# First batch's plain value rows loaded as float32 by SyncE and cast by VectorE, with the plain heads' products and the first FFN tiles reordered

## The chip, the cores and the metric

The kernel runs on one core of a Trainium2 chip. The time is the device time in microseconds of that core. A profile of one execution stands beside it; its span, 311.4 us, runs from the first to the last instruction and is a little shorter than the time. The granted TensorE clock was 1.000 throughout.

## The reference

Eight batches of windowed attention over 576 tokens, eight heads of 64; the first four heads ("plain") see the last 32 tokens, the other four ("dilated") every fourth of the last 128. The result, laid out as tokens by 512, goes through a two-layer network with a squared ReLU.

```python
B, H, S, D = q.shape                      # 8, 8, 576, 64
scores = scale * np.matmul(q, k.transpose(0, 1, 3, 2))
rel = pos[:, None] - pos[None, :]
mask_plain = (rel >= 0) & (rel < 32)
mask_dil = (rel >= 0) & (rel < 32 * 4) & (rel % 4 == 0)
masks = np.stack([mask_plain if h < H // 2 else mask_dil for h in range(H)], axis=0)
attn = softmax(np.where(masks, scores, -1e9))
x = np.matmul(attn, v).transpose(0, 2, 1, 3).reshape(B * S, H * D)   # 4608 x 512
h = np.maximum(x @ w_in, 0.0)             # 512 x 2048
out = (h * h) @ w_out                     # 2048 x 512
```

All inputs and outputs are float32. The kernel computes in bf16 with float32 sums.

## The kernel before

All of the order is fixed by hand. A string, PROGRAM, lists small steps; a "|" stands for the next FFN group. Heads are taken in pairs e: pairs 0 and 1 are plain, 2 and 3 dilated. The first batch is cut into part 0 (tokens 0 to 255) and part 1 (256 to 575). For pair e and part p the steps are: T transposes q and k on TensorE, C copies them out of PSUM, B starts an accumulator with the mask's bias, S adds the scores, E takes the exponential on ScalarE, P multiplies with the values, D sums the denominators, L and X take their logarithm and the exponential of its negative on ScalarE, M multiplies into xT on VectorE. "w9" and "W2" are matmuls on idle operands that keep TensorE occupied. "L0:" codes are loads of the first batch by GpSimd: q (with k), v in parts, i0 to i3 the four pieces of w_in, o0 to o3 those of w_out.

```python
PROGRAM = (
    "L0:q001 L0:q023 L0:q101 L0:q123 L0:v0d L0:v0p L0:i0 L0:v1dr L0:i1 L0:v1p L0:i2 L0:i3 L0:o0 L0:o1 L0:o2 "
    "L0:o3 L1:q00123 z y L1:v0dp L1:q10123 L1:v1dpr w9 T00 C00a T10 C10a B00 B10 S00 E00 B20 S10 E10 B30 T20q "
    "B01 W2 T20k C20v T30 C30v B11 W1 S20 E20 W1 S30 E30 T01 C01v T11 C11v W1 S01 E01 T21 C21v B21 S11 E11 T31 "
    "C31v P20 P30 D20 D30 L20 X20 M20 P00 P10 D00 D10 L00 X00 M00 B31 S21 E21 S31 E31 W2 | | P21 P31 D21 D31 "
    "L21 X21 M21 L31 X31 M31 | | P01 P11 D01 D11 L01 X01 M01 L11 X11 M11 | | | | | | | | | | | | | m n | | | | "
    # ... later batches
)
```

The values of the first batch. "p" are those of the plain heads, cast by the DMA into their places in `vbd`; "d" those of the dilated heads; "r" the last 64 tokens of the dilated heads.

```python
def load_v(b: int, parts, which="pdr"):
    dst = vbd[b % 2]
    # ...
    for what in which:
        if what == "p":
            for e in range(NE // 2):
                for hl, rows in sides:
                    nc.gpsimd.dma_start(                                   # L178
                        dst[rows, e, i0:i1, rows],
                        v[b, 2 * e + hl, 64 * i0 : 64 * i1, :].rearrange("(i p) d -> p i d", p=64),
                    )
        # ... "d" into vds (L184)
        elif p1 == 2:
            for hl, rows in sides:
                nc.gpsimd.dma_start(                                       # L197
                    dst[rows, NE // 2 : NE, 8, rows],
                    v[b, H // 2 + hl : H : 2, 512:S, :].rearrange("h p d -> p h d"),
                )
```

The first layer of the FFN. A tile of 256 tokens has eight accumulators u, each of eight matmuls (two column blocks, four rows kt of x; row kt is pair kt). Accumulators 0 and 1 need piece 0 of w_in, 2 and 3 piece 1, and so on. Accumulators, score banks and some products share the four PSUM buffers of `ps_f`. The h2T step takes ReLU on ScalarE and squares on VectorE.

```python
def ffn_groups(tk0: int, nt: int):
    early = 0 < tk0 <= 2 * NT
    # ...
    kts = (0, 2, 1, 3) if tk0 >= NT else (2, 3, 0, 1)
    cut = 3 if tk0 >= NT else 2

    def mm1(u, ks):
        if u not in acc:
            acc[u] = ps_f.tile([P, NT], f32, name="pf")
        # ... matmuls of the rows ks                                         L668
        hv = h2[:, per * u : per * u + per, 0:nt]
        nc.scalar.activation(hv, acc[u][:, :].rearrange("p (x n) -> p x n", x=per), ACT.Relu)   # L679
        nc.vector.tensor_tensor(out=hv, in0=hv, in1=hv, op=ALU.mult)                             # L680

    def g1(i):
        if i < 2 and early:
            for u in (2 * i, 2 * i + 1):
                mm1(u, kts[:cut])
        elif i < 4 and early:
            for u in (2 * i - 4, 2 * i - 3):
                mm1(u, kts[cut:])
        else:
            mm1(i, kts)
    # ... g2: the second layer (L700), copy to osb (L706), store by SyncE (L642)

head = groups[:G]        # 0..15: tile 0 (tokens 0-255), 16..31: tile 1 (tokens 256-511)
groups[:NF] = [head[y] for y in (0, 1, 2, 3, 16, 17, 18, 19, 4, 5, 20, 21, 6, 7, 22, 23)]
```

Of the kernel before, what the change touches and what calls it, by code (L numbers as in the profile page):

```python
# [21 lines left out]
    "L0:q001 L0:q023 L0:q101 L0:q123 L0:v0d L0:v0p L0:i0 L0:v1dr L0:i1 L0:v1p L0:i2 L0:i3 L0:o0 L0:o1 L0:o2 "  # L22
    "L0:o3 L1:q00123 z y L1:v0dp L1:q10123 L1:v1dpr w9 T00 C00a T10 C10a B00 B10 S00 E00 B20 S10 E10 B30 T20q "
    "B01 W2 T20k C20v T30 C30v B11 W1 S20 E20 W1 S30 E30 T01 C01v T11 C11v W1 S01 E01 T21 C21v B21 S11 E11 T31 "
    "C31v P20 P30 D20 D30 L20 X20 M20 P00 P10 D00 D10 L00 X00 M00 B31 S21 E21 S31 E31 W2 | | P21 P31 D21 D31 "
    "L21 X21 M21 L31 X31 M31 | | P01 P11 D01 D11 L01 X01 M01 L11 X11 M11 | | | | | | | | | | | | | m n | | | | "
    "| L2:q00123 L2:q10123 | 1q1 1q3 | 1q2 1k2 | 1k1 1v3 | 1a2 | 1v2 1k0 1q0 | 1o2 | 1a0 1a1 | 1k3 1o0 1o1 | "
    "1a3 1Q0 | 1K0 1o3 | 1Q1 1K1 | 1Q2 | 1b0 | | 1Q3 1K2 L2:vwpdr L3:q00123 L3:q10123 | L2:x | | 2q0 | | 2k0 "
    "1V2 | 1b2 1p0 | 1b1 1V3 1K3 | | 1p2 1p1 | 2a0 1b3 | 2k1 2o0 2b0 1p3 | 2q1 2k2 L3:x | | 2q2 2p0 L3:vwpdr "
    "2a1 | | | 2b1 | 2o1 2q3 2a2 | | 2p1 2v2 | 2k3 | 2b2 2o2 | 2v3 | 2a3 2p2 L4:q10123 | 2b3 3k1 | 2o3 3q1 | | "  # L30
    "3a1 L4:q00123 2p3 | 3k0 3k2 | | 3o1 | | | 3q0 3v2 | | | | 3a0 | 3b1 3k3 | | | 3p1 L4:x 3q2 L4:vwpdr | | "  # L31
    "3b0 | 3a2 3q3 3o0 4k0 | | | 3o2 3b2 | | 3p0 3v3 | 4q1 3a3 | 3p2 4q2 4q0 | L5:q10123 3b3 | 3o3 | 4k1 | | "
# [31 lines left out]
def kernel(  # L64
# [9 lines left out]
    nc = tc.nc  # L74
    P = nc.NUM_PARTITIONS
    B, H, S, D = q.shape
# [378 lines left out]
    first = {}  # L455
    sides = [slice(64 * hl, 64 * hl + 64) for hl in range(2)]

    def turn(n: int, cols: int):


        if "W" not in first:
            pool, nm = (ps_f, "pf") if ("P", 2, 0) in first else (ps_o, "po")
            first["W"] = pool.tile([P, 512], f32, name=nm)
        for _ in range(n):
            nc.tensor.matmul(
                first["W"][:, 0:cols], idle[:, 0:P],
                idle[:, 0:256].unsqueeze(1).broadcast_to([P, cols // 256, 256]), start=True, stop=True, skip_group_check=True
            )

    def first_step(code: str):  # L470
# [91 lines left out]
        elif what == "P":  # L562
            if ("P", *pair) not in first:
                if pair in ((2, 0), (2, 1), (0, 1)):
                    od = ps_o.tile([P, 512], f32, name="po"), ps_d.tile([P, 512], f32, name="pd")
                else:
                    od = [ps_a.tile([P, 512], f32, name="pa") for _ in range(2)]
                first.pop("W", None)
                first["P", *pair] = od
# [75 lines left out]
    def ffn_groups(tk0: int, nt: int):  # L645
# [3 lines left out]
        early = 0 < tk0 <= 2 * NT  # L649
        h2 = h2_pool.tile([P, NF, NT], bf16, name="h2T")  # L650
        per = NT // nt
        kts = (0, 2, 1, 3) if tk0 >= NT else (2, 3, 0, 1)
# [29 lines left out]
        def g1(i):  # L682
            if i < 2 and early:
                for u in (2 * i, 2 * i + 1):
                    mm1(u, kts[:cut])
            elif i < 4 and early:
# [4 lines that stand above are left out]
# [76 lines left out]
    def run(code):  # L767
# [7 lines left out]
        elif code == "m":  # L775
            masks()
        elif code == "n":
            zero_halves(kbd)
            zero_halves(vbd[0][:, NE // 2 :, 0:8, :])
        elif code[0] in "wW":  # L780
            turn(int(code[1:]), 512 if code[0] == "w" else 256)
# [26 lines left out]
    groups[:NF] = [head[y] for y in (0, 1, 2, 3, 16, 17, 18, 19, 4, 5, 20, 21, 6, 7, 22, 23)]  # L808
# [54 lines left out]
```

## Time and profile before

| | |
|---|---|
| time, median of 3 | 313.79 us (313.38 to 313.93) |
| span in the profile | 311.4 us |
| TensorE busy | 300.0 us, 96% |
| ScalarE, VectorE busy | 196.9 us, 193.7 us |
| GpSimd busy | 96.3 us, nearly all of it issuing loads |
| second layer's first matmul (L700) starts | 35.07 us |

A timeline line gives the start, the time from the start to the end of a run of like instructions, the engine, the source line, the operation with its operands and shape, the count, and in brackets how long the engine had been idle just before and what ended that idleness. A matmul's end is modelled, so starts are the thing to compare. GpSimd's load lines are the issues alone. The landings of the first loads, from the trace's DMA answer (issue plus time to landing):

| load | KB written | issued, us | landed after, us |
|---|---|---|---|
| q, first | 128 | 1.25 | 3.3 |
| q, third load (pairs 2, 3) | 128 | 2.60 | 5.1 |
| k of pairs 2, 3, part 1 (eighth) | 160 | 5.70 | 6.1 |
| plain values, part 0, first of four | 32 | 7.99 | 4.8 |
| w_in piece 0 (fifteenth) | 512 | 11.41 | 5.7 |
| w_in piece 1 | 512 | 14.48 | 6.9 |
| w_in piece 2 | 512 | 18.68 | 7.4 |
| w_in piece 3 | 512 | 19.71 | 9.0 |

### The profile page before, as it was taken

The page shows a single profiled execution, that of the slowest core. Times are in us where ns is not written, and L with a number is a line of the kernel's source. Part 1 is how long each engine was busy: PE and PEld are TensorE (multiplying, and loading weights), DVE is VectorE, ACT ScalarE, POOL GpSimd, SP SyncE. Part 2 cuts the span into 40 slices and gives each one's busy share as a digit, 9 for nine tenths or more (in the row PEclk, how much of TensorE's full clock was granted, in tenths as well). Part 3 has the DMA queues.
Part 4 walks back from the last instruction along what each step waited for, and adds up shares of the span by engine and source line. Part 5 has one row for each costly group of instructions (what it writes and reads, how often), then busy time and mean ns, then how long its engine had stood idle before and what let it go on. Part 6 is the DMA issues. An engine that isn't in the chain of part 4 may idle for free.

```text
span 311.4 us, 6742 instructions
## 1 busy us (share of the span) xinstructions
PE 300.0 (96%) x2532; PEld 186.1 (60%) x2564; DVE 193.7 (62%) x631; ACT 196.9 (63%) x420; POOL 96.3 (31%) x142
## 2 busy tenths in 40 slices
PE   7989999999999999999999999999999999999994
PEld 3769746968755555565599555555555555445443
DVE  1445567998978879974898469946994334104400
ACT  7377738859878865785388547854786456226511
POOL 8879785664236254501451041000000000000000
PEclk9999999999999999999999999999999999999999
DMA  8999999999999969999699976502200210121022
GB/s 108 153 182 211 206 148 180 174 127 221 153 101 194 175 107 204 155 101 199 98 132 115 173 126 90 101 10 61 67 2 1 69 68 0 36 67 34 2 67 67
DMA packets 79808, 34.91 MB, mean 112 GB/s; under 512 B 49824, under 2 KB 74784, under 8 KB 79776
## 3 DMA queue, kind: packets, MB, share of 16 engines
q0 software_dynamic: 47680, 18.36, 53.4%
q1 hardware_dynamic: 31952, 15.93, 28.8%
q8 instruction: 20, 0.33, 0.5%
q10 hardware_dynamic: 144, 0.20, 0.2%
q14 instruction: 12, 0.10, 0.2%
HBM read 36.90 MB, written 9.44 MB: 149 GB/s over the span
## 4 chain that ended last, share of the span: by engine, by line
PE 81%; ACT 5%; DMA 5%; DVE 2%; POOL 2%; issue 2%; SPq 0%; ACTq 0%; POOLq 0%
PE pf L668 36%; PE pf L700 36%; PE po L413 3%; PE pd L415 2%; DMA w_in<-in_moe_w_in_dram 2%; DMA qb<-in_q_dram 2%; PE pa L304 2%; ACT h2T L679 1%; PE pa L310 1%; ACT qT L248 1%; DMA out_dram<-osb 1%; PE pa L235 1%; ACT osb L706 1%; DVE xT L428 1%; DVE kbd L252 1%
## 5 line engine op out<-in xcount | busy, mean ns | idle before, releaser
L668 PE MATMUL pf<-xT,w_in 128*128 128x256 bf16 (+1 forms) x758 | 132.7, 325 | 2.9 <-DMA w_in<-in_moe_w_in_dram 1.4
L700 PE MATMUL pf<-w_out_sb,h2T 128*128 128x512 bf16 (+1 forms) x570 | 130.9, 373 | 1.7 <-ACT osb L706 0.5
L668 PEld LDWEIGHTS <-w_in 128*128 128x128 bf16 x768 | 82.3, 114 | 38.3 <-issue 1.9
L679 ACT ACTIVATE h2T<-pf 128x512 bf16<-128x512 f32 x144 | 83.8, 598 | 25.1 <-PE pf L668 24.2
L700 PEld LDWEIGHTS <-h2T 128*128 128x128 bf16 x592 | 54.3, 98 | 53.9 <-issue 0.7
L680 DVE TENSOR_TENSOR h2T<-h2T 128x512 bf16<-128x512 bf16 x144 | 58.1, 423 | 41.5 <-ACT h2T L679 39.9
L706 ACT COPY osb<-pf 128x512 f32<-128x512 f32 (+1 forms) x37 | 21.2, 572 | 42.2 <-PE pf L700 42.1
L428 DVE TENSOR_TENSOR xT<-po,rec 128x288 bf16<-128x288 f32 (+2 forms) x52 | 23.7, 456 | 30.5 <-ACT rec L418 30.0
L178 POOL DMA_DIRECT2D vbd<-in_v_dram x40 | 28.2, 725 | 43.0 <-PE pd L415 39.6
L417 ACT ACTIVATE rec<-pd 128x288 f32<-128x288 f32 (+2 forms) x52 | 21.5, 413 | 24.0 <-PE pd L415 21.5
L314 ACT ACTIVATE pt<-pa 128x352 bf16<-128x352 f32 (+6 forms) x56 | 27.6, 499 | 8.4 <-PE pa L310 4.7
L418 ACT ACTIVATE rec<-rec 128x288 f32<-128x288 f32 (+2 forms) x56 | 24.9, 444 | 1.8
L413 PEld LDWEIGHTS <-vbd 128*128 128x128 bf16 x286 | 16.8, 97 | 9.9 <-issue 0.7
L248 DVE COPY qT<-xx 64x288 bf16<-64x288 bf16 x80 | 19.4, 243 | 1.8 <-DMA xx<-qb 0.7
L191 POOL DMA_DIRECT2D vd<-in_v_dram x24 | 14.6, 624 | 15.1 <-DMA kb<-in_k_dram 8.1
L252 DVE COPY kbd<-xx 64x288 bf16<-64x288 bf16 x40 | 18.8, 470 | 0.6
L161 POOL DMA_DIRECT2D qb<-in_q_dram x18 | 13.0, 720 | 18.8 <-DMA xx<-qb 17.1
L413 PE MATMUL po<-pt,vbd 128*128 128x96 bf16 (+3 forms) x263 | 18.0, 199 | 0.3 <-DVE vbd L207 0.2
L415 PE MATMUL pd<-pt,mk 128*128 128x96 bf16 (+5 forms) x158 | 16.3, 203 | 0.0
L197 POOL DMA_DIRECT2D vbd<-in_v_dram x16 | 9.6, 608 | 12.3 <-PE pd L415 5.1
L161 POOL DMA_DIRECT2D kb<-in_k_dram x18 | 12.8, 709 | 2.0 <-PE pf L415 1.1
L304 PE MATMUL pa<-qT,kbd 128*128 128x96 bf16 (+2 forms) x146 | 12.2, 201 | 0.5 <-ACT qT L248 0.5
(82 smaller groups left out, 230.4 us busy)
## 6 DMA issues: line engine op xcount, KB each, us to landing
out_dram<-osb SPq DMA_DIRECT2D x18, 128.0 KB, 3.4
qb<-in_q_dram POOLq DMA_DIRECT2D x7, 320.0 KB, 7.3
kb<-in_k_dram POOLq DMA_DIRECT2D x7, 320.0 KB, 8.0
vd<-in_v_dram POOLq DMA_DIRECT2D x32, 64.0 KB, 6.2
w_in<-in_moe_w_in_dram POOLq DMA_DIRECT2D x4, 512.0 KB, 7.2
w_out_sb<-in_moe_w_out_dram POOLq DMA_DIRECT2D x4, 512.0 KB, 12.9
qb<-in_q_dram POOLq DMA_DIRECT2D x7, 256.0 KB, 7.0
kb<-in_k_dram POOLq DMA_DIRECT2D x7, 256.0 KB, 8.7
```

The source lines that it names most:

```text
L161: nc.gpsimd.dma_start(t[0:n, part, hs, :], src[b, hs, t0 : t0 + RES * n, :].rearrange("h (p r) d -> p h (r d)", r=RES))
L178: nc.gpsimd.dma_start(dst[rows, e, i0:i1, rows], v[b, 2 * e + hl, 64 * i0 : 64 * i1, :].rearrange("(i p) d -> p i d", p=64),)
L314: nc.scalar.activation(pt[:, off : off + n], ps[:, 0:n], ACT.Exp, scale=SCALE)
L413: nc.tensor.matmul(oo, vb[:, e, i, :], rh, start=(x == 0), stop=(x == len(mms) - 1), skip_group_check=True)
L415: nc.tensor.matmul(dd, ones[:, :], rh, start=(x == 0), stop=(x == len(dms) - 1), skip_group_check=True)
L418: nc.scalar.activation(rec[:, 0:n], rec[:, 0:n], ACT.Exp, scale=-1.0)
L428: nc.vector.tensor_tensor(out=tok, in0=o if o is o3 else o[:, 0:n], in1=rec if o is o3 else rec[:, 0:n], op=ALU.mult)
L668: nc.tensor.matmul(acc[u][:, nt * x + y0 : nt * x + y1], w_in_sb[piece][:, kt, c0 : c0 + 509 : 4], xT[:, kt, t0 : t0 + y1 - y0], start=(kt ...
L679: nc.scalar.activation(hv, acc[u][:, :].rearrange("p (x n) -> p x n", x=per), ACT.Relu)
L680: nc.vector.tensor_tensor(out=hv, in0=hv, in1=hv, op=ALU.mult)
L700: nc.tensor.matmul(cur[m][:, c0:c1], h2[:, f, P * m : P * m + P], w_out_sb[:, f, c0:c1], start=(f == 0), stop=(f == NF - 1),)
L706: nc.scalar.copy(osb[:, c0:c1], cur[m][:, c0:c1])
```

## The change

The plain heads' values of the first batch, and the last 64 tokens of the dilated heads, no longer come through GpSimd's queue with a cast. SyncE, which has nothing to do until the first stores at 41 us, loads them as float32 into the three `osb` buffers that later hold output rows, and VectorE casts them into `vbd`. A tiny memset on VectorE ahead of each set fixes when the loads may start. With the ten issues out of GpSimd's queue, w_in moves ahead in it. Since the plain values are meant to be there early, the plain heads' products of part 0 (P00 ... M00) are taken before those of the dilated ones. The first two FFN tiles follow suit: each one's first two accumulators are filled with two rows of x first and the other two in the next group, tile 0 in the order plain, dilated, tile 1 in the order dilated, plain.

```diff
-    "L0:q001 L0:q023 L0:q101 L0:q123 L0:v0d L0:v0p L0:i0 L0:v1dr L0:i1 L0:v1p L0:i2 L0:i3 L0:o0 L0:o1 L0:o2 "
-    "L0:o3 L1:q00123 z y L1:v0dp L1:q10123 L1:v1dpr w9 T00 C00a T10 C10a B00 B10 S00 E00 B20 S10 E10 B30 T20q "
-    "B01 W2 T20k C20v T30 C30v B11 W1 S20 E20 W1 S30 E30 T01 C01v T11 C11v W1 S01 E01 T21 C21v B21 S11 E11 T31 "
-    "C31v P20 P30 D20 D30 L20 X20 M20 P00 P10 D00 D10 L00 X00 M00 B31 S21 E21 S31 E31 W2 | | P21 P31 D21 D31 "
-    "L21 X21 M21 L31 X31 M31 | | P01 P11 D01 D11 L01 X01 M01 L11 X11 M11 | | | | | | | | | | | | | m n | | | | "
+    "L0:q001 L0:q023 L0:v0d L0:q101 L0:q123 L0:i0 L0:v1d L0:i1 L0:i2 L0:i3 L0:o0 L0:o1 L0:o2 L0:o3 L1:q00123 z "
+    "y L1:v0dp L1:q10123 L1:v1dpr w9 T00 C00a g0 T10 C10a B00 B10 S00 E00 B20 S10 E10 B30 W2 T20q T20k C20v "
+    "T30 C30v h0 W3 S20 E20 W1 S30 E30 P00 P10 D00 D10 L00 X00 T01 C01v g1 M00 T11 C11v B01 B11 P20 P30 D20 "
+    "D30 L20 X20 M20 S01 T21 C21a T31 C31v E01 S11 E11 | B21 S21 E21 h1 | B31 S31 E31 P21 P31 D21 D31 L21 X21 "
+    "M21 L31 X31 M31 P01 P11 D01 D11 L01 X01 M01 L11 X11 M11 | | | | | | | | | | | | | | | m n | | | | | "
 # ... later batches: the same steps, wrapped elsewhere
+    plain = {}
+    def load_plain(part: int):                       # codes g0, g1
+        if part == 0:
+            plain[0] = t = osb_pool.tile([P, DM], f32, name="osb")
+            nc.vector.memset(t[:, 0:512:256], 0.0)
+            to = [t[:, 256 * e : 256 * e + 256] for e in range(2)]
+        else:
+            plain[1] = ts = [osb_pool.tile([P, DM], f32, name="osb") for _ in range(2)]
+            for t in ts:
+                nc.vector.memset(t[:, 0:448:64], 0.0)
+            to = [t[:, 0:320] for t in ts]
+            for hl, rows in enumerate(sides):
+                nc.sync.dma_start(
+                    ts[0][rows, 320:448].rearrange("p (h d) -> p h d", d=D),
+                    v[0, H // 2 + hl : H : 2, 512:S, :].rearrange("h p d -> p h d"),
+                )
+        for e in range(2):
+            for hl, rows in enumerate(sides):
+                nc.sync.dma_start(
+                    to[e][rows, :].rearrange("p (i d) -> p i d", d=D),
+                    v[0, 2 * e + hl, 256 * part : 256 + 320 * part, :].rearrange("(i p) d -> p i d", p=64),
+                )
+    def cast_plain(part: int):                       # codes h0, h1
+        for rows in sides:
+            if part == 0:
+                x = plain[0][rows, :].rearrange("p (e i d) -> p e i d", e=2, d=D)
+                nc.vector.tensor_copy(vbd[0][rows, 0:2, 0:4, rows], x)
+            else:
+                x = plain[1][0][rows, 320:448].rearrange("p (e d) -> p e d", d=D)
+                nc.vector.tensor_copy(vbd[0][rows, 2:4, 8, rows], x)
+                for e in range(2):
+                    x = plain[1][e][rows, 0:320].rearrange("p (i d) -> p i d", d=D)
+                    nc.vector.tensor_copy(vbd[0][rows, e, 4:NB, rows], x)
 # ... the idle matmuls (W) always in ps_o
-                    od = [ps_a.tile([P, 512], f32, name="pa") for _ in range(2)]
+                    pool, nm = (ps_a, "pa") if part else (ps_f, "pf")
+                    od = [pool.tile([P, 512], f32, name=nm) for _ in range(2)]
-        early = 0 < tk0 <= 2 * NT
+        early = NT <= tk0 <= 2 * NT
-        kts = (0, 2, 1, 3) if tk0 >= NT else (2, 3, 0, 1)
+        kts = (0, 2, 1, 3) if tk0 >= NT else (0, 1, 2, 3) if tk0 == 0 else (2, 3, 0, 1)
         def g1(i):
-            if i < 2 and early:
+            if i < 2 and tk0 < NT:
+                for u in range(2):
+                    mm1(u, kts[2 * i : 2 * i + 2])
+            elif i < 2 and early:
-    groups[:NF] = [head[y] for y in (0, 1, 2, 3, 16, 17, 18, 19, 4, 5, 20, 21, 6, 7, 22, 23)]
+    groups[:NF] = [head[y] for y in (0, 1, 16, 2, 3, 17, 18, 19, 4, 5, 20, 21, 6, 7, 22, 23)]
```

In the built programs nothing else moves: after the head each engine has the same instructions in the same order, GpSimd has ten issues fewer, SyncE ten more, VectorE three memsets and eight casts more, and the copy C21 goes from VectorE to ScalarE.

## The prediction

> **What bounds the kernel now.** I read the page first, then stretches of five microseconds, then TensorE's timeline and the chain of waits of the first 45 us. The page's engine table and its row of slices show where there is anything to win.
>
> ```profile
> PE 300.0 (96%) x2532; PEld 186.1 (60%) x2564; DVE 193.7 (62%) x631; ACT 196.9 (63%) x420; POOL 96.3 (31%) x142
> ...
> PE   7989999999999999999999999999999999999994
> ```
>
> TensorE is busy 96% of 311.4 us at full clock, and from 100 to 300 us, which the change leaves alone, the stretches give it 99.31 and 99.40 of each 100 us. The first 35 us are what can change; they end where the first second-layer matmul (L700) starts, at 35.07 us. TensorE's timeline from 15 us (start, duration, then in brackets the idle time before and who ended it):
>
> ```profile
> 15.89 0.39 PE L465 MATMUL pf<-idle 128*128 128x256 bf16 x2
> 17.14 2.16 PE L668 MATMUL pf<-xT,w_in 128*128 128x256 bf16 x16 [0.85 <-DMA w_in<-in_moe_w_in_dram]
> 19.23 0.46 PE L587 MATMUL po<-pt,vd 64*64 64x32 bf16 x16
> ...
> 21.45 1.94 PE L668 MATMUL pf<-xT,w_in 128*128 128x256 bf16 x16 [0.53 <-DMA w_in<-in_moe_w_in_dram]
> ...
> 26.45 8.79 PE L668 MATMUL pf<-xT,w_in 128*128 128x256 bf16 x79 [0.30 <-DVE xT L620]
> 35.07 6.21 PE L700 MATMUL pf<-w_out_sb,h2T 128*128 128x512 bf16 x27
> ```
>
> Two waits are for pieces of the first weight (0.85 and 0.53 us), one for x (0.30). Before 15 us there are gaps of 0.26, 0.20, 0.30 and 0.18 us and seven idle-operand fillers worth about 0.2 us each. Together some 4 us, 1.3% of the run, is the most that any reordering here can give. From 26.45 to 41 us TensorE does not wait: 79 matmuls in 8.62 us, 0.109 us each.
>
> GpSimd's timeline says why the weights are late:
>
> ```profile
> 9.14 1.83 POOL L178 DMA_DIRECT2D vbd<-in_v_dram  x3 [0.52 <-DMA kb<-in_k_dram]
> 11.41 0.76 POOL L752 DMA_DIRECT2D w_in<-in_moe_w_in_dram  x1 [0.44 <-DMA qb<-in_q_dram]
> ```
>
> Its queue reuses eight semaphores, so each load waits for the landing of the one eight places earlier (the program's waits show it). Piece 0 of w_in is the fifteenth load, is issued at 11.41 us and lands 5.7 us later, at 17.1. The DMA answer for 2 to 22 us, in half-microsecond slices, shows the queues starving ahead of it:
>
> ```profile
> GB/s 264 59 83 187 188 120 84 77 114 152 171 168 174 185 180 186 193 190 198 136 92 40 35 53 205 209 205 209 190 180 203 199 198 209 207 172 151 154 143 167
> ```
>
> From 12 to 14 us the rate is 92, 40, 35 and 53 GB/s, against 205 next to it. Part of that is the plain values' 128-byte packets; I put the rest, a true hole, at 1.3 us. Otherwise the queues are full from 2.5 us to the end of the weights, so order in the stream decides landings.
>
> **What the Trainium skill says.** "DMA: Bandwidth & Descriptors", section "SWDGE vs HWDGE vs iDMA": a cast in a DMA is to be had on GpSimd only; hence float32 staging and a VectorE cast. Its section "Issuing engines are not separate DMA queues" says that all issuers share the same 16 engines and interleave, so a second queue saves issue time only. The profile before has no SyncE load beside GpSimd's to test it, but it fits the full stream. "VectorE: DVE Perf Modes", "The perf-mode tier table": a float32 SBUF copy of 2048 elements takes 1227 ns, twice the plain rate; my estimate for 512 is 0.43 us (0.27 of streaming and 0.16 fixed). No such copy is in the trace. "SBUF — State Buffer", "SBUF: two separate sides", warns that such a copy locks GpSimd out of writing descriptors; here it could delay only issues that are already ahead of the stream.
>
> **Part by part.** *Loads.* Ten GpSimd issues go (8 of 725 ns, 2 of 608 ns in the page's means: 7.0 us). w_in piece 0 becomes the eleventh load and waits for the third, which lands 5.1 us after 2.60: issue at about 7.7 us instead of 11.41, and the hole closes. In exchange SyncE brings the same values as float32: 256 KB in four loads and 384 KB in six, twice the written bytes, in 256-byte packets. The first four start after a VectorE memset behind the first k copy (6.4 us). Before, only the first set stood ahead of piece 0; the second set came after piece 1. Now the second set is issued at about 13 us by my chain below and shares the engines with piece 0's last part. Landing of piece 0: 17.1 - 1.3 (hole) + 0.3 (wider writes) = 16.1 us, up to 0.6 more if the second set gets in.
>
> *Attention's first part.* To the last plain exponentials nothing moves; scores of pairs 2 and 3 end at about 10.5 us. P00 then needs both casts. The fourth SyncE load is issued near 8 us; with the 2.3 us that the mask load on ScalarE's queue takes alone, and some sharing, it lands near 10.6, and two casts of 0.43 us end at 11.3: a new wait of 0.8 us. P00 to D10 take 0.62 (as at 14.23 before), L00 and X00 1.2 on ScalarE, M00 0.7: x of the plain heads is there at 13.9 us instead of 17.55. T01, T11, B01, B11, pairs 2 and 3's products, S01, T21, T31 and S11 follow, 3.4 us of TensorE work with small waits: the first FFN group is ready at about 15.3 us. So it waits for the weight, and t = 16.1.
>
> *From t on.* The first two groups now hold 16 matmuls (rows 0,1 then 2,3 of two accumulators): 1.75 us. Between and after stand B21, S21, B31, S31 (1.3), the products and sums of pairs 2 and 3 (19.23 to 20.73: 1.5) and of 0 and 1 (23.22 to 24.12: 0.9). Then comes tile 1's first group, which needs rows 2,3 of x: M21 and M31. Two waits arise. ScalarE takes E31 after two squaring inputs h2T, so P31 waits 0.3 us. And L21, X21, L31, X31, M31 take 2.3 us from D21's end (20.73 to 23.02 before), while TensorE has only D31 and the 0.9 us of P01 to D11: it waits about 1.4 us. Before, two FFN groups (1.94 us) stood in that place. So t + 1.75 + 1.3 + 1.5 + 0.9 + 0.3 + 1.4 = t + 7.15 to tile 1's first group, then 112 matmuls at 0.109 = 12.2, and 0.2 for an accumulator bank: t + 19.5. Break-even with 35.07 is t = 15.6; with t = 16.1 the mark is reached at 35.6, 0.5 us later. After that the order is unchanged and TensorE full, so the shift is kept: 313.79 + 0.5 = 314.3 us.
>
> **Rivals.** (1) Piece 0 lands as early as TensorE is ready, 15.3 us or before, because the queues' packets overlap better than in one queue; then the mark is 34.8 or less. If the 1.4 us behind M31 is also smaller, 1 to 1.5 us are won: 312.4. For it speaks the hole and the fact that x of plain heads comes 3.6 us earlier; against it, 640 KB of float32 ahead of or beside piece 0, where before 128 KB of bf16 stood ahead of it. (2) The SyncE loads are slow among the full queues: the fourth lands at 12, P00 starts at 12.8, q and k of part 1 land a microsecond later too, and t becomes 17: 315.2. For it: out stores of 128 KB took 5.9 us to land in this stretch. (3) The head is only exchanged, TensorE being short of w_in piece 1 either way (0.53 us before): then nothing, 313.8. Against it: piece 1's first use moves behind tile 1's group, to about t + 8, after 24 us, and its landing (21.4 before) leaves slack.
>
> **Range and chances.** t may lie between 15.1 and 17.1 and the waits behind it may be off by 0.6, which gives about 34.0 to 36.7 for the mark; the run-to-run spread (313.38 to 313.93) adds little. I lean a little to the early side, since I may have put the loads too strictly in line: 312.8 to 315.5. Two per cent is 6.3 us; only 4 us can be won, and losing 6 would need TensorE to stand still for all that the loads can be late. So within 2%: 0.98, 0.01 on each side.
>
> **What would show it.** First L668 between 15.3 and 17 us, its idle time ended by w_in; P00 waiting for VectorE's cast; no slice under 100 GB/s between 12 and 14 us; tile 1's first group waiting for the multiply of M31 (an idle of over 1 us ended by VectorE); the first L700 at 35.6. Wrong if the first L668 starts before 15, if P00 follows S30 at once, or if a stretch after 40 us differs by more than 0.3 us.

## The result and the profile after

| | before | after |
|---|---|---|
| time, median of 4 | 313.86 us (313.38 to 314.21) | 336.90 us (335.85 to 337.27) |
| span in the profile | 311.4 us | 335.0 us |
| mean granted TensorE clock | 1.000 | 0.979 |
| second layer's first matmul starts | 35.07 us | 58.42 us |

The change makes the kernel slower: the ratio is 1.073, with a 95% interval of 1.0702 to 1.0758. The prediction was 314.3 us (312.8 to 315.5) and was wrong by 22.6 us. The span grew by 23.6 us, and the mark at which the second layer starts moved by 23.35 us. So nearly all of the loss is made ahead of that mark, where the prediction had placed what can change.

The page of the changed kernel: the engine table, and the rows of 40 slices (one is 8.4 us) for TensorE and for its granted clock.

```profile
PE 310.5 (93%) x2563; PEld 191.7 (57%) x2563; DVE 197.6 (59%) x641; ACT 198.0 (59%) x421; POOL 90.1 (27%) x132
...
PE   8375289999999999999999999999999999999995
PEclk9999569999999999999999999999999999999999
```

TensorE's busy share falls to 3, 7, 5 and 2 tenths in slices 2 to 5 (8.4 to 42 us), where it had been 8 or 9. In the fifth and sixth slice the clock is at five and six tenths.

TensorE's timeline of the changed kernel, 18 to 59 us (start, time to the end of the run, engine, line, operation, count; in brackets the idle time before and who ended it):

```profile
18.53 0.77 PE L627 MATMUL pf<-pt,vbd 128*128 128x96 bf16 x8 [6.87 <-DVE vbd L486]
...
25.38 1.89 PE L708 MATMUL pf<-xT,w_in 128*128 128x256 bf16 x8
...
29.58 0.44 PE L627 MATMUL po<-pt,vd 64*64 64x32 bf16 x16
39.84 0.23 PE L627 MATMUL po<-pt,vbd 128*128 128x64 bf16 x1 [9.82 <-DVE vbd L489]
...
42.84 0.56 PE L627 MATMUL po<-pt,vbd 128*128 128x32 bf16 x6 [1.13 <-DVE xT L660]
...
44.41 14.17 PE L708 MATMUL pf<-xT,w_in 128*128 128x256 bf16 x112
58.42 1.89 PE L743 MATMUL pf<-w_out_sb,h2T 128*128 128x512 bf16 x8
```

Two waits stand out. P00 waits 6.87 us and P21 waits 9.82 us, each for a cast of values that SyncE loads (L486 is the cast of the first set, L489 that of the dilated rows in the second, L492 that of its plain rows). Before, neither waited at all:

```profile
14.23 0.48 PE L587 MATMUL pa<-pt,vbd 128*128 128x96 bf16 x8
...
19.76 0.19 PE L587 MATMUL po<-pt,vbd 128*128 128x64 bf16 x1
```

The first FFN group (25.38) waits for nothing: w_in is there by then. From the start of the 112 matmuls at 44.41 to the mark it is 14.01 us, where the prediction had 12.2: they begin at half speed.

A cast is short. VectorE's timeline shows that it is itself kept waiting, by the load:

```profile
16.89 0.42 DVE L486 CAST vbd<-osb 64x512 bf16<-64x512 f32 x1 [6.55 <-DMA osb<-in_v_dram]
18.05 0.42 DVE L486 CAST vbd<-osb 64x512 bf16<-64x512 f32 x1 [0.73 <-DMA osb<-in_v_dram]
21.28 0.08 DVE L467 MEMSET osb<- 128x7 f32 x2
29.55 0.22 DVE L489 CAST vbd<-osb 64x128 bf16<-64x128 f32 x1 [3.68 <-DMA osb<-in_v_dram]
36.34 0.48 DVE L492 CAST vbd<-osb 64x320 bf16<-64x320 f32 x1 [6.57 <-DMA osb<-in_v_dram]
39.05 0.48 DVE L492 CAST vbd<-osb 64x320 bf16<-64x320 f32 x1 [2.23 <-DMA osb<-in_v_dram]
39.56 0.22 DVE L489 CAST vbd<-osb 64x128 bf16<-64x128 f32 x1
```

P21 itself needs only the dilated rows, the two casts of L489. Their loads had landed by 31.8 us, but the second of these casts stands behind two of L492 in VectorE's order, and those wait for the plain rows, which landed between 36.3 and 40.4 us. That order is not what costs the time: P01, two products later, needs the plain rows anyway. e1 below shows it: there P21 goes 2.76 us earlier, P01 waits longer, and the mark does not move.

The chain of work that ended last, in order of time (start, duration, what), says the same from the other side:

```profile
8.95 9.00 DMA osb<-in_v_dram
...
21.38 0.59 SPq L470
...
24.05 14.91 DMA osb<-in_v_dram
```

One load of the first set takes 9.00 us and one of the second 14.91 us. These two stretches are 23.9 us of the first 40. They also stand in line: the memsets that start the second set (L467, at 21.28 in the timeline above) lie behind x copies that need TensorE, and TensorE had stood until 18.53. So the second set is issued at 21.38 us; the prediction had it at about 13.

Are the DMA engines idle meanwhile? The DMA answer of the changed kernel for 0 to 45 us (40 slices of 1.125 us, then the median time from issue to landing):

```profile
GB/s 0 57 148 173 125 117 174 164 148 154 192 206 190 189 196 204 207 206 207 206 209 230 199 223 209 211 217 203 219 202 190 182 183 184 184 160 152 173 135 171
...
osb<-in_v_dram SPq DMA_DIRECT2D x4, 80.0 KB, 14.6
...
osb<-in_v_dram SPq DMA_DIRECT2D x4, 64.0 KB, 8.2
```

They are not: from 11 to 34 us they move 189 to 230 GB/s. The hole that the prediction wanted closed is closed. What they move, though, is mostly something else than the 640 KB that everyone waits for.

### The profile page after: what moved, and what is told of

Same layout as the page of the kernel before. It is cut to its first block, busy times and chain, and to the rows that moved or that the text cites. A ratio compares the mean times of both kernels' runs of the same rounds, so it can differ in the third digit from the quotient of the medians.

```text
span 335.0 us, 6792 instructions
## 1 busy us (share of the span) xinstructions
PE 310.5 (93%) x2563; PEld 191.7 (57%) x2563; DVE 197.6 (59%) x641; ACT 198.0 (59%) x421; POOL 90.1 (27%) x132
## 4 chain that ended last, share of the span: by engine, by line
PE 80%; DMA 7%; ACT 5%; DVE 4%; issue 2%; SPq 1%; ACTq 0%; DVEq 0%
PE pf L708 35%; PE pf L743 34%; DMA osb<-in_v_dram 7%; PE po L413 3%; PE pd L415 2%; PE pa L304 2%; PE po L505 1%; PE pa L310 1%; ACT h2T L719 1%; ACT qT L248 1%; PE pa L235 1%; SPq L476 1%; DVE kbd L252 1%; DVE xT L428 1%; ACT rec L417 1%
## 5 line engine op out<-in xcount | busy, mean ns | idle before, releaser
L708 PE MATMUL pf<-xT,w_in 128*128 128x256 bf16 (+1 forms) x768 | 136.2, 331 | 0.6 <-DVE xT L428 0.3
L743 PE MATMUL pf<-w_out_sb,h2T 128*128 128x512 bf16 (+1 forms) x592 | 134.5, 373 | 0.5 <-ACT osb L749 0.5
L708 PEld LDWEIGHTS <-w_in 128*128 128x128 bf16 x768 | 83.3, 115 | 37.4 <-issue 1.2
L749 ACT COPY osb<-pf 128x512 f32<-128x512 f32 (+1 forms) x37 | 21.2, 573 | 42.2 <-PE pf L743 40.0
L178 POOL DMA_DIRECT2D vbd<-in_v_dram x32 | 23.1, 742 | 77.8 <-PE pd L415 57.3
L413 PEld LDWEIGHTS <-vbd 128*128 128x128 bf16 x286 | 16.9, 97 | 10.2 <-issue 1.0
L248 DVE COPY qT<-xx 64x288 bf16<-64x288 bf16 x80 | 20.1, 251 | 1.1
L304 PE MATMUL pa<-qT,kbd 128*128 128x96 bf16 (+2 forms) x146 | 12.2, 201 | 0.5 <-ACT qT L248 0.5
L627 PEld LDWEIGHTS <-vbd 128*128 128x128 bf16 x22 | 1.7, 131 | 18.3 <-DVE vbd L489 9.9
## 6 DMA issues: line engine op xcount, KB each, us to landing
w_in<-in_moe_w_in_dram POOLq DMA_DIRECT2D x4, 512.0 KB, 11.7
```

Of the source, the lines that this page charges most:

```text
L178: nc.gpsimd.dma_start(dst[rows, e, i0:i1, rows], v[b, 2 * e + hl, 64 * i0 : 64 * i1, :].rearrange("(i p) d -> p i d", p=64),)
L248: copy(qT[rows, e, :, m0 : m0 + n].rearrange("p (c j) m -> p j c m", j=2)[:, jj, :, :], src)
L413: nc.tensor.matmul(oo, vb[:, e, i, :], rh, start=(x == 0), stop=(x == len(mms) - 1), skip_group_check=True)
L708: nc.tensor.matmul(acc[u][:, nt * x + y0 : nt * x + y1], w_in_sb[piece][:, kt, c0 : c0 + 509 : 4], xT[:, kt, t0 : t0 + y1 - y0], start=(kt ...
L743: nc.tensor.matmul(cur[m][:, c0:c1], h2[:, f, P * m : P * m + P], w_out_sb[:, f, c0:c1], start=(f == 0), stop=(f == NF - 1),)
```

## The theories

**Theory of turns.** The DMA engines serve SyncE's queue and GpSimd's in turn, one packet each. SyncE's packets are of 256 bytes. GpSimd's are of 512 bytes for q and k (59 ns each in the trace), 1024 for w_in (96 ns) and 4096 for w_out (322 ns). While GpSimd's queue is full of long packets, SyncE gets a small part of the bandwidth, and its 1024 and 1536 packets take as long as that many long ones do. The Trainium skill, "DMA: Bandwidth & Descriptors", section "Queues, rings and completion order", says that an engine goes round its queue rows and switches at packet boundaries, a packet being typically 9 to 17 descriptors. The trace agrees with the going round. Its records of the two queues come in equal numbers (counted below), and evenly: from 36 to 38 us every tenth of a microsecond holds 20 to 28 of SyncE's and 22 to 26 of GpSimd's. That fits a step of a single record, which this document calls a packet; the records do not name their engine, so the order on one engine is inferred.

**Rivals.** (A) A SyncE load of this form is slow in itself, whatever stands beside it. (B) The new order of the products is what costs. (C) TensorE's half speed in the first 45 us is what costs, and the waits only hide it.

## The experiments

Where no ratio is given, the time is that of one execution.

**e1: the weights later.** The two steps that clear buffers on GpSimd ("z y") come before the first piece of w_in, so that the first set meets no weights.

```diff
-L0:q123 L0:i0 L0:v1d L0:i1 ... L1:q00123 z y L1:v0dp
+L0:q123 z y L0:i0 L0:v1d L0:i1 ... L1:q00123 L1:v0dp
```

> Only GpSimd's order is changed: its 9.6 us of memsets (z and y) come before the first weight load, so that the first set of SyncE's value loads meets only q, k and v loads (512-byte packets) and no w_in packets (1024 bytes). Theory A (on each DMA engine SyncE's queue and GpSimd's take turns packet by packet, so a SyncE load lasts as many turns as it has packets, each turn as long as one packet of each queue): 64 packets per engine at about 70 ns a turn instead of 113, so the first set is over about 3.5 to 4 us earlier and TensorE's wait before P00 falls from 6.87 us to 3 us or less. The second set still meets w_in and w_out, so a long wait before the second plain products stays, and the time is 330 to 337 us. Theory B (SyncE's loads of 64-partition float32 rows are slow of themselves, about 7 us for a set of four, whatever else is queued): the wait before P00 stays at 6 to 7 us.

Measured: 336.71 us, the same time. The first set lands earlier, its last packet at 14.1 us instead of 17.4 (counted in the trace), and between 12.0 and 12.5 us, when GpSimd's queue runs dry, SyncE's packets come at 674 per us, against 142 beside w_in in the changed kernel. That fits turns. Yet P00 began only 0.96 us earlier, at 17.57 us, after a wait of 7.53 us. GpSimd's and VectorE's timelines of this run show why:

```profile
14.26 1.80 POOL L813 MEMSET kb<- 16x2048 bf16 x1
16.01 1.22 POOL L814 MEMSET kb<- 16x1024 bf16 x1
```

```profile
14.61 2.90 DVE L486 CAST vbd<-osb 64x512 bf16<-64x512 f32 x2 [5.16 <-DMA osb<-in_v_dram]
```

Two casts that take 0.42 us each elsewhere took 2.90 us together, and they end just behind GpSimd's memsets. The Trainium skill, "SBUF — State Buffer", section "SBUF: two separate sides", describes an exclusive lock on the port pair that the two engines share; the prediction had feared it for GpSimd's issues only. So most of what the earlier landing won went into a new collision. (These memsets are in the kernel before too, six of them from 24.62 to 34 us; GpSimd's busy time there is not issues alone.) The second set met w_out as before. P21 waited 9.41 us, and P01 behind it another 4.99, since the last plain rows landed at 42.2 us:

```profile
43.95 0.56 PE L627 MATMUL po<-pt,vbd 128*128 128x32 bf16 x6 [4.99 <-DVE xT L660]
```

The mark is at 58.66 us, against 58.42.

**e2: wide packets.** SyncE reads four (part 0) or five (part 1) rows of a head as one run of 1024 or 1280 bytes. The values then stand in other places of the buffers than the products read, so the run tells only of times.

```diff
-v[0, 2 * e + hl, 256 * part : 256 + 320 * part, :].rearrange("(i p) d -> p i d", p=64)
+v[0, 2 * e + hl, 256 * part : 256 + 320 * part, :].rearrange("(p i) d -> p i d", p=64)
```

> SyncE loads the same number of bytes of the plain values, but each partition takes four (five) neighbouring tokens, so runs are 1024 and 1280 bytes instead of 256: 16 packets per engine instead of 64 in the first set, 32 instead of 96 in the second. The plain values then stand in wrong places, so the output is not the reference's; every instruction and byte count is as in the changed kernel. Theory A (turns): the first set lasts 16 turns of about 0.2 us, 3 us instead of 7, the wait before P00 falls to 2 to 3 us, the second set lasts 6 to 8 us instead of 14, and the time falls to 317 to 325 us. Theory B (SyncE's loads slow of themselves, or bytes decide): waits of about 6.9 and 9.8 us stay and the time is 335 to 338 us.

Measured: 331.23 us. The waits fell to 5.11 and 9.05 us only, and neither theory's time came. In the second set turns hold: from 29 to 32 us the 1280-byte packets came at 39 to 42 per us against 43 to 47 of w_out's, where the changed kernel had about 50 per us of 256 bytes. Five times the bytes in a packet took a fifth off the count, so the shares go by packets and not by bytes. The expected 6 to 8 us were too short for a set that meets w_out: 512 packets are 32 turns on each of 16 engines. With the packet times of the trace (322 ns for w_out's, 31 and 68 for SyncE's two sizes) that is an estimate of 11.9 us, and the set took 11.7, from 23.6 to 35.3. But the first set's packets came more slowly than one to one (17 to 64 per us against 152 to 268 of GpSimd's, from 10 to 15 us), which turns alone do not explain. Part of the first wait is therefore something else; a late start of the first packets is one piece of it (below).

**e3: SyncE first.** Both sets are issued at the very start of the program.

```diff
-w9 T00 C00a g0 T10 ... C01v g1 M00
+g0 g1 w9 T00 C00a T10 ... C01v M00
```

> Both sets of SyncE's loads are started at the very beginning (their memsets first on VectorE), ahead of nearly all of GpSimd's loads. Theory A (turns): 160 packets per engine against 512-byte packets, about 70 ns a turn, so all are in by 12 to 13.5 us, long before the weights' packets; q and k come about 1 us later. Both waits for casts vanish (under 1 us each), TensorE stays warm, and the time is 313.5 to 317 us. Theory B (slow of themselves): the ten loads need some 17 to 20 us from the start, a wait of 5 us or more before the second plain products stays and the time is above 320 us.

Measured: 317.94 us, ratio to before 1.0132 (1.0081 to 1.0183). Both large waits are gone. The first line of SyncE's timeline (the ten issues run to 7.9 us) and VectorE's casts in this run:

```profile
1.06 2.76 SPq L476 DMA_DIRECT2D osb<-in_v_dram  x4
```

```profile
11.02 0.97 DVE L486 CAST vbd<-osb 64x512 bf16<-64x512 f32 x2
...
18.45 0.86 DVE L492 CAST vbd<-osb 64x320 bf16<-64x320 f32 x2
```

No cast waits for its load. The same ten loads, with the same 256-byte packets, land 3.8 to 9.4 us after their issue, most of them beside q and k. That is against rival A in its strict form, and 19 of the 23 us go with the time at which the loads run. Some 4 us stay.

**e4: the new order without SyncE's loads.** GpSimd loads the plain values with a cast, as before the change: the first set ahead of piece 0 of w_in, the second behind piece 1.

```diff
-L0:q123 L0:i0 L0:v1d L0:i1 L0:i2 ... g0 ... g1 ... h0 ... h1
+L0:q123 L0:v0p L0:i0 L0:v1dr L0:i1 L0:v1p L0:i2 ...
```

> The new order of products and FFN groups is kept, but the plain values come again by GpSimd with the cast (first set behind q and k and ahead of w_in piece 0, second set behind piece 1), with no SyncE loads and no VectorE casts. If the loads are the whole loss: no waits of several microseconds, and by the prediction's own sum with w_in piece 0 at 17.1 us the mark is 36.5 us, so 314 to 316 us. If the new order costs by itself (tile 1's first group behind M31, two-row groups): 318 us or more.

Measured: 320.61 us, ratio 1.0207 (1.0158 to 1.0255), with two waits for those loads in P00:

```profile
13.51 0.45 PE L627 MATMUL pf<-pt,vbd 128*128 128x96 bf16 x4 [1.78 <-DMA vbd<-in_v_dram]
15.06 0.45 PE L627 MATMUL pf<-pt,vbd 128*128 128x96 bf16 x4 [1.10 <-DMA vbd<-in_v_dram]
```

So the new order needs the plain values earlier than GpSimd's queue can bring them. Rival B is worth at most the 7 us of this run, not 23. TensorE was at half speed from 5 to about 24 us in this execution, which makes the rest of its loss hard to divide.

**b1: the kernel before, once more.**

> The kernel before once more, unchanged, for a second profile of its first 12 us. In its first profile the transposes of pair 0 took 0.31 us from 4.83 us on (full speed), in the profiles of the changed kernel and of four variants of it 0.42 us (about half the clock), with the same nine starting fillers in front. If the speed at the start differs by chance from execution to execution, this profile may show 0.42 too and the time is still about 313 to 316 us; if the programs differ in it by something systematic, it shows 0.31 again, and 313 to 314 us.

Measured: 316.44 us, while its neighbours on the same chip ran at 313.24 to 315.07. In this execution the transposes took 0.42 us instead of 0.31 and kept that until about 20.5 us; the second layer began at 37.82 us instead of 35.07. The first transposes before, and below them those of b1:

```profile
4.83 0.31 PE L496 MATMUL pa<-mk,qb 64*64 64x64 bf16 x8
```

```profile
5.02 0.42 PE L496 MATMUL pa<-mk,qb 64*64 64x64 bf16 x8
```

How soon TensorE reaches full speed at the start thus differs from execution to execution of one kernel, and was worth 2.75 us here. All that follows below about 3 us must be read with this in mind.

**e5: keeping TensorE occupied during the waits.** 62 idle matmuls before P00 and 90 before P21 in the changed kernel.

```diff
-E30 P00 ... S31 E31 P21
+E30 W62 P00 ... S31 E31 W90 P21
```

> The changed kernel with idle-operand matmuls put into its two long waits: 62 of 256 columns before P00 (6.8 us at full clock) and 90 before P21 (9.8 us). Nothing else changes, and the waits for the casts remain. If the two idle stretches cost extra because TensorE comes out of them at half clock: the 112 first-layer matmuls take 12.2 us instead of 14.2, the work after each wait runs at full speed, and the time falls by 4 to 8 us, to 329 to 333 us. If the half clock has nothing to do with the idle stretches: 336 to 338 us.

Measured: 337.08 us, no gain. TensorE's timeline:

```profile
17.87 0.49 PE L627 MATMUL pf<-pt,vbd 128*128 128x96 bf16 x8 [1.12 <-DVE vbd L486]
...
39.88 0.24 PE L627 MATMUL po<-pt,vbd 128*128 128x64 bf16 x1 [3.96 <-DVE vbd L489]
```

Here TensorE was at full speed until the fillers ended (the 90 took 10.00 us, 0.111 each, up to 35.4 us), and P21 still began at 39.88 us, against 39.84. Its speed before that point decides nothing; SyncE's second set does. That ends rival C as the main cause. The fillers ended 3.96 us too soon, and what followed was at half speed again: from the start of the 112 matmuls to the mark it was 14.01 us, as in the changed kernel. What that half speed behind P21 costs, this run therefore does not tell; e8 does.

**e6: e3 with more idle matmuls at the start** ("w13" for "w9").

> SyncE's loads first, as in e3_sync_first (317.94 us), and 13 instead of 9 full-width fillers at the start (1.7 us more at half clock). If what e3 still loses is half clock in the first 14 us and the fillers start the full clock earlier: pairs' transposes at 0.31 us, and 314 to 316.5 us although the first of them begins up to 1.5 us later. If the fillers have no hold on the clock: 318 to 320 us.

Measured: 317.85 us (315.82 to 320.04), ratio 1.0146 (1.0073 to 1.022). The four times were 315.95, 320.04, 319.75 and 315.82, two by two, so the fillers are no sure hold on the clock. The profiled execution was one of the two shorter, at full speed from the first transpose, and can be held directly against the profile of before:

```profile
15.27 0.33 PE L535 MATMUL pa<-mk,kb 80*64 80x80 bf16 x8 [1.08 <-DMA kb<-in_k_dram]
17.58 1.06 PE L708 MATMUL pf<-xT,w_in 128*128 128x256 bf16 x8 [1.32 <-DMA w_in<-in_moe_w_in_dram]
21.62 0.46 PE L627 MATMUL pa<-pt,vd 64*64 64x32 bf16 x16 [0.29 <-ACT pt L600]
23.98 0.39 PE L627 MATMUL po<-pt,vbd 128*128 128x32 bf16 x6 [1.33 <-DVE xT L660]
25.03 12.39 PE L708 MATMUL pf<-xT,w_in 128*128 128x256 bf16 x112
37.26 6.21 PE L743 MATMUL pf<-w_out_sb,h2T 128*128 128x512 bf16 x28
```

The mark is at 37.26, 2.19 us behind before's 35.07, and the time of these two executions is 2.2 us above before's median on that chip (313.66). So of e3's 4 us about 2 belong to what one sees here. TensorE waits for k and for w_in, which land later beside SyncE's early packets: the last k of the first batch at 15.2 us instead of 13.2 in the changed kernel, which has the same order in GpSimd's queue, and piece 0 of w_in at 17.5 instead of 16.6. And P01 waits 1.33 us for M21 (L660): both use the one PSUM buffer `po`, and P01 may not write it before M21 has read it. The other 2 go with the two longer executions; the speed at the start is the likely cause, but neither of them was profiled.

**e7: the kernel before without its nine idle matmuls at the start.**

> The kernel before without its nine starting fillers, all else the same: what half clock at the start costs in the old order. If the full clock in the first 17 us is worth much there too, 316 to 321 us, with transposes of 0.42 us; if the old order hides a slow TensorE behind its waits for w_in, 313 to 315 us.

Measured: 317.06 us; half speed until about 21 us and the mark at 37.91, nearly as in b1, which had the nine.

**e8: both sets together.** The second set is issued right behind the first, from about 9.4 us, in place of 21.38, so that it meets w_in and not w_out.

```diff
-C00a g0 T10 ... C01v g1 M00
+C00a g0 g1 T10 ... C01v M00
```

> The changed kernel with the second set of SyncE loads issued directly behind the first (both from 6.7 us on) instead of at 21.4 us. Theory of turns (one SyncE packet of 256 bytes per GpSimd packet): the 1536 packets of the second set now meet q, k and w_in, about 140 to 235 packets per us, and are in by 28 to 29.5 us; P21, which is otherwise ready at about 30, waits at most 0.5 us instead of 9.82; the first set lands within 1 us of before (17.8 us); the first second-layer matmul starts at 47 to 50 us and the time is 326 to 330. Rival (the first set's wait and half-speed TensorE at the start carry the loss, the second set being only a follower): time stays over 333.

Measured: 322.45 us, 14.45 us less than the changed kernel, for moving one code. TensorE's timeline:

```profile
17.83 0.77 PE L627 MATMUL pf<-pt,vbd 128*128 128x96 bf16 x8 [7.64 <-DVE vbd L486]
...
28.06 0.20 PE L627 MATMUL po<-pt,vbd 128*128 128x64 bf16 x1 [0.85 <-DVE vbd L492]
...
31.61 12.39 PE L708 MATMUL pf<-xT,w_in 128*128 128x256 bf16 x112
43.84 1.46 PE L743 MATMUL pf<-w_out_sb,h2T 128*128 128x512 bf16 x5
```

The second set's last packet came at 26.8 us and the wait fell from 9.82 to 0.85 us. The gain is larger than the 7 to 11 us expected. The mark moved by 14.58 us, in three parts. The wait is 8.97 us shorter. The way from P21 to the mark takes 15.78 us instead of 18.58, 2.80 less: without the long idle TensorE stays at full speed. And TensorE is ready for P21 2.81 us sooner: this execution ran its first transposes at full speed, P00 began 0.70 us earlier, and full speed was back at 21.7 us instead of about 27. That the moved code brought this last part is not shown; b1 has such a difference between two executions of one kernel. The second set's late landing is thus worth 11.8 us, and at most 14.6.

**e9: w_out last.** SyncE's loads stay where the change has them in the program; GpSimd's loads for the second batch, with short packets, and its buffer clearing ("z y") go ahead of w_out.

```diff
-L0:i3 L0:o0 L0:o1 L0:o2 L0:o3 L1:q00123 z y L1:v0dp L1:q10123 L1:v1dpr
+L0:i3 L1:q00123 z y L1:v0dp L1:q10123 L1:v1dpr L0:o0 L0:o1 L0:o2 L0:o3
```

> The changed kernel with GpSimd's loads of the second batch (packets of 128 and 512 bytes) put ahead of the four pieces of w_out (4096 bytes); SyncE's loads are issued where the change has them. Theory of turns: the second set, issued at about 21.4 us and starting to move at about 25, meets packets of 0.03 to 0.1 us instead of 0.32 us, so its 1536 packets come at 150 or more per us and are in at 31 to 35 us; the wait of P21 falls from 9.82 us to 1 to 5 us. Rival (a SyncE load of this form takes its 8 to 15 us whatever stands beside it): wait of P21 9 us or more, landing at about 39. The time itself is left open: w_out comes later and may set the start of the second layer.

Measured: 330.12 us. The four larger loads of the second set land 4.5 us (median) after their issue instead of 14.6, and P21 waits 1.09 us. This is the cleanest test of rival A: the same loads, from the same place in the program and also late, differ by a factor of three with what stands in the other queue. (From 28 to 30 us SyncE's came at 490 to 545 per us against 370 to 379, most of them of 128 bytes, so the other queue was empty on some engines for part of that time.) The first set's casts now fell beside GpSimd's memsets and took 1.99 us each, so P00 waited 12.12 us and the second set was issued only at 24.74 us. That is the collision of e1 a second time:

```profile
17.52 2.01 POOL L817 MEMSET vbd<- 64x2304 bf16 x1
19.48 2.08 POOL L813 MEMSET qb<- 16x2048 bf16 x1
```

```profile
17.84 4.00 DVE L486 CAST vbd<-osb 64x512 bf16<-64x512 f32 x2 [8.65 <-DMA osb<-in_v_dram]
```

**e10: the loads alone, in the old order.** The kernel before with the ten SyncE loads at the start of the program and VectorE's casts where they fit: the first set before P20, the second behind E31.

```diff
-L0:v0d L0:v0p L0:i0 L0:v1dr L0:i1 L0:v1p L0:i2 ... w9 T00 ... C31v P20 ... S31 E31 W2
+L0:v0d L0:i0 L0:v1d L0:i1 L0:i2 ... g0 g1 w9 T00 ... C31v h0 P20 ... S31 E31 h1 h2 W2
```

> The loads part alone: the order of products and FFN groups of the kernel before, the plain values and the last 64 dilated rows by SyncE as float32 from the very start of the program (as in the run with both sets at the start, 317.94), casts on VectorE where they fit. If the 4 us that remained there belong to the new order of products (its waits of 0.75, 0.29 and 1.33 us and its cold start), this takes 313 to 315.5, first second-layer matmul at 34.5 to 36.5 us. Rival (the SyncE packets' share of the engines delays q, k and w_in wherever it stands): 317 to 319. Faster than 312.5 is expected by neither.

Measured: 318.65 us, ratio 1.0121 (1.0044 to 1.0199). The expectation of 313 to 315.5 failed: the remaining 4 us do not belong to the new order alone. The profiled execution, the second longest of the four (319.91), has its mark at 41.35 us. It was at half speed until 22 us; two casts of 64x128 that take 0.22 us elsewhere took 3.89 us together from 22.56 us, where GpSimd's memsets begin (22.27), and P21 waited 1.06 us for them.

**e11: only the first set by SyncE.** The kernel before, with four SyncE loads at the start and the cast before P20.

```diff
-L0:v0d L0:v0p L0:i0 ... w9 T00 ... C31v P20
+L0:v0d L0:i0 ... g0 w9 T00 ... C31v h0 P20
```

> The kernel before with only the four plain loads of part 0 taken over by SyncE at the very start of the program (cast by VectorE before P20); part 1 stays with GpSimd, the order of the products too. The four SyncE loads land by 7 us, no wait for their casts; w_in piece 0 is issued near 8 us instead of 11.41, so the waits of 0.85 and 0.53 us for w_in before the first two groups go. If what remained in the run with both sets (318.65) came from the second set's casts beside GpSimd's memsets (L489 1.9 us each, 1.06 us of wait) and from TensorE's slow start, this takes 312.5 to 314.5. Rival (the SyncE packets beside q and k at the start hold TensorE back in its first 8 us and so keep it at half speed for longer): 316 to 319, transposes at 0.42 us until 15 us or later.

Measured: 318.36 us, ratio 1.0112 (1.0065 to 1.0159); all six times lie between 317.17 and 319.01, where eleven of before went from 313.04 to 316.56. The number is the rival's. TensorE's timeline of e11, and below it some of the same steps in b1, the slow start of before:

```profile
6.20 0.31 PE L535 MATMUL pa<-mk,kb 64*64 64x64 bf16 x8 [0.62 <-DMA kb<-in_k_dram]
...
8.42 0.42 PE L535 MATMUL pa<-mk,qb 64*64 64x64 bf16 x8
...
16.13 0.48 PE L535 MATMUL pa<-mk,qb 80*64 80x80 bf16 x8
...
18.45 0.77 PE L626 MATMUL pa<-pt,vbd 128*128 128x96 bf16 x8 [0.47 <-DVE vbd L486]
```

```profile
16.12 0.48 PE L496 MATMUL pa<-mk,qb 80*64 80x80 bf16 x8
...
17.76 0.79 PE L587 MATMUL pa<-pt,vbd 128*128 128x96 bf16 x8
```

The delay that the rival named is there. The first k lands at 6.15 us, where it lands at 5.22 before and 5.36 in b1, and TensorE, at full speed so far, waits 0.62 us for it; e3 (0.63) and e10 (0.59), which also issue SyncE's loads first, have this wait too. From 8.42 us on TensorE runs at half speed. At 16.13 against 16.12 us it is level with b1, which was at half speed from the start. From there e11 loses 0.69 us up to P00, with 0.47 of it as a wait for the cast; its mark is at 38.77, 0.95 behind b1's and 3.70 behind the first profile of before. So this execution, the shortest of the six (317.17), is behind by the 2.75 us of b1's slow start and another 0.95; the other five took 0.2 to 1.8 us longer and were not profiled. Whether the wait for k brings the half speed on, or whether six of six is chance, stays open.

No variant tried beats the kernel before.

**Turns, counted.** From the packet records of the traces, full packets that began in one microsecond, all 16 engines together:

| run and stretch | GpSimd's packets | their time | GpSimd per us | SyncE (256 bytes) per us |
|---|---|---|---|---|
| e3, 5 to 8 us | 512 bytes | 59 ns | 233 | 233 |
| after, 36 to 38 us | 512 bytes | 59 ns | 242 | 235 |
| e8, 19 to 25 us | 1024 bytes (w_in) | 96 ns | 153 | 151 |
| after, 26 to 33 us | 4096 bytes (w_out) | 322 ns | 48 | 50 |
| e1, 12.0 to 12.5 us | hardly any | 59 ns | 42 | 674 |

Nearly one to one, whatever the size, and much more when the other queue is dry. Of the 1536 packets of the second set in the changed kernel only 434 had begun by 34 us, although the first began at 25.3; once w_out was nearly through, the other 1102 took 5.9 us. For the first set turns give an estimate of 5.8 to 8.1 us (64 on each of 16 engines, of 31 ns and 59 to 96 ns); its packets took 6.7 us, from 10.7 to 17.4. The 3.9 us between its first issue and its first packet come on top, and turns do not explain them.

## Why the prediction was wrong, point by point

- **The new wait for the first casts, "0.8 us": this is where it failed first.** The step said that the fourth SyncE load, issued near 8 us, lands near 10.6, from the 2.3 us of the mask load and "some sharing". It was issued at 8.95 and landed 9 us later; the wait was 6.87 us. The mask load had run in an empty machine (its packets were through at 2.9 us, when GpSimd's first had hardly begun); these ran beside a full queue. Of the 11.2 us from the set's first issue to its last landing, 3.9 passed before the first packet and 6.7 with packets in turn. Rival 2 of the prediction named the mechanism ("slow among the full queues") and sized it at 1.4 us for the whole.
- **The second set: the largest term, and it was not in the sum.** The prediction used the set only as a burden on w_in, issued at about 13 us, and gave its own landing no line. It was issued at 21.38, behind the first wait, and had its last packet at 39.9; P21 waited 9.82 us. With the half speed that this idle leaves behind, it costs 11.8 to 14.6 us of the mark (e8).
- **The sum as a ladder.** After 336.90; with the second set moved ahead 322.45 (14.45 less); with the first set also at the start 317.94 (4.51 less); before 313.86 (4.08 less). Of the last step about 2 us are the waits for k, for w_in and of P01 in e6, and about 2 probably the speed at the start. The times come from different groups of runs, and 322.45 is a single execution, so a step may be off by up to 3 us (b1).
- **"All issuers share the same 16 engines and interleave, so a second queue saves issue time only": right for the total, and misread.** The total rate was 189 to 230 GB/s from 11 to 34 us. But I took interleaving to mean fair shares of bytes or order of issue. It was one packet each, and so the queue with the short packets came off badly.
- **w_in piece 0 issued at 7.7 us and the hole closed: right.** It was issued at 7.50 us, and no slice lies under 100 GB/s between 12 and 14 us. It landed 9.1 us later, at 16.6 us; predicted 16.1.
- **First FFN group at 16.1 us, waiting for w_in: wrong in the changed kernel (25.38 us, no wait), 1.5 us early for a kernel whose values are there in time.** In e6 it starts at 17.58 us after a wait of 1.32 us for w_in.
- **"t + 19.5" from there to the mark: right in size, in part by luck.** In e6 it is 37.26 - 17.58 = 19.68 us. Its parts: the wait for E31 0.29 (predicted 0.3), a wait behind the multiplies 1.33 (1.4), the 112 matmuls 12.23 from their start to the mark (12.2). But the second wait is not the one described. The prediction let tile 1's first group wait for M31; it is P01 that waits, for M21 and the buffer `po`, and the group then follows without a wait, because M31 has ended at 24.76 us, 0.27 before it. In the changed kernel the 112 matmuls took 14.01 us, in part at half speed.
- **The cast of 0.43 us: right where it runs alone, 0.42.** Beside GpSimd's memsets it took up to 1.99 (e9).
- **After the head the shift is kept: right**, 23.35 us at the mark and 23.6 in the span.
- **The chances.** They rested on the bound that TensorE would have to stand still "for all that the loads can be late". That bound was never worked out. The trace of before held a number for it: w_in, sharing a full queue, took 5.7 to 9.0 us to land. Two sets in line at that rate would have been a warning of more than 10 us. The upper end of the range was also added up short: 17.1 + 19.5 + 0.6 is 37.2 us for the mark, not 36.7. It changes nothing here.

## What to carry to other kernels

Moving a load to a second queue takes it out of one line and puts it into a race, and there its share is counted in packets: beside a queue of long packets, many short packets were slow here however few bytes they held. So size such a load by its number of packets times the packet time of its neighbour, and start it while the neighbour's packets are short or its queue is empty. And follow each new load to the instruction that waits for it, the late ones too: a load whose issue hangs behind another wait adds its own latency to it.

## What the runs showed of the hardware that I had not expected

- About one 256-byte packet of SyncE's queue goes for each packet of GpSimd's, at 233, 151 and 50 per us beside packets of 512, 1024 and 4096 bytes.
- The first packet of a SyncE load can come late: 3.9 us after the issue in both sets of the changed kernel (3.1 to 4.0 in e1, e2, e5 and e8), against 1.6 us for the loads at the start of the program (e3). A full queue beside it is not enough for that: in e9's second set it was 1.8 us, although GpSimd's 512-byte packets came at about 300 per us. Why was not tried.
- A float32 cast of 64x512 on VectorE goes from 0.42 to 1.99 us beside GpSimd's memsets.
- The clock record is no full account of TensorE's speed: in the changed kernel, transposes at 20 us take 0.47 us and P00 0.77, against 0.31 and 0.48 before, while the record for 18 to 23 us is 1.00.
